# Attention and two MoE layers on one core: a third score group moved ahead, row gathers spread out, the last three feed-forward chunks grouped by tile

## The chip, the core and the metric

The kernel runs on one NeuronCore of a Trainium2 chip. Its engines work side by side, each on a queue of its own: TensorE (PE, matmuls; its weight loads are listed as PEld), VectorE (DVE), ScalarE (ACT), GpSimd (POOL) and SyncE (SP, which here only issues DMAs). Matmuls write into eight PSUM banks; DVE and ACT bring results from there to SBUF. The metric is the device time of one execution in microseconds (us); less is better. All times below are us unless marked ns.

## What is computed

Three stages follow one another. The inputs are q, k, v of 2 x 8 x 768 x 64, weights of 8 experts, and the two matrices of a feed-forward layer.

```python
# attention: a band of |i - j| < 16 beside 24 block summaries of 32 keys each
k_sum = k.reshape(B, H, nb, 32, D).max(axis=3)
v_sum = v.reshape(B, H, nb, 32, D).mean(axis=3)
scores_l = where(|i - j| < 16, scale * q @ k.T, -1e9)
scores_s = scale * q @ k_sum.T + log(32)
a = softmax(concat([scores_l, scores_s]))
x = (a @ concat([v, v_sum])).transpose(0, 2, 1, 3).reshape(1536, 512)
# experts: each row goes to the one expert with the largest logit
e = argmax(x @ w_gate, axis=1)
x = gate_w[:, None] * (relu(x @ w1[e]) @ w2[e])     # 512 -> 1024 -> 512
# feed-forward: 512 -> 2048 -> 512
h = x @ w_in
out = maximum(0.01 * h, h) @ w_out
```

## The kernel before

Products that need full precision are made of two rounded halves: an operand is split into a high part (cast on ACT) and a low part (the difference, on DVE), and three matmuls (high-high, high-low, low-high) replace one.

*Attention.* The 16 heads are worked as 8 pairs, each in two groups of six 64-row query tiles, so 16 groups n. A group runs through `scores` (PE: mask L325, products L337), `rowmax` (DVE L347), `weights` (ACT, exponentials L359), `turn_a` and `take_a` (PE transposes L368, ACT copy L372), `values` (PE L382) and `put_x` (DVE L394 to L405: division and the logits). Beside them, per pair, `project` (PE L305) makes the share of the logits that comes from the values, `project_t` transposes it (copy L309, transposes L313, copy L316), `mean_v` (PE L287) makes the block means of v, and `spread_v` (ACT L294) copies them behind each query tile's values. No loop sets the order. Each step is entered into a list `plan` with a due time (tables STAGE, EARLY and ONCE, L56 to L125, in units of one pair = 2), the list is sorted, and the steps are issued in that order; every engine works its own part of it in order.

*The first experts' rows.* `pick_rank`, `pick0` (L484 to L493), `pick1` to `pick3` and `pick_hot` choose, once the first 768 rows are known, the rows of the first two expert blocks (256 rows each); `pick_id` (L552) turns them by a matmul (L555) into a tile of row numbers `tid0` (DVE cast L558); `pick_x` (L560) gathers 128 rows each from the DRAM copy `xrows` with an indirect DMA (L561). All row copies into `xrows` (`put`, L417) and all gathers are issued by POOL. `b_turn` transposes the gathered rows of block 0; `b_l10` and `b_l11` are its first two units.

*The expert blocks.* A `Block` (L603) works on 256 rows of one expert, in eight units f of the hidden size: `load` (SP), `split` into halves, `layer1(f)` (L664, then ACT L670 and DVE L671), `layer2(f)` (L684), and at the end `store` (ACT L691, DVE L692). The first block has its order written out in the string POST (L130). Into it are mixed the five steps of `sort()`, which counts the rows of each expert (L803), finds each row's place (L820 to L827, one-hots L829 to L837), and turns that into the row numbers `tid` (PE L846, DVE cast L847), and then gathers all twelve tiles of 128 sorted rows (L849 to L857; L852 is the DMA). `list` works out which expert each later block has (L872 to L925), `zero` fills (L1116) the still unused part of x2h and x2l. From block 1 on `block()` (L1151) runs: in each unit it places two gathered tiles, `place` (L956), by PE transposes (L700) and copies, until all twelve are placed.

*Feed-forward.* Two halves of 768 rows, 16 chunks of the hidden size each, 32 chunks i in all. `ff1(i)` (L1233) makes the hidden chunk (L1243) and splits it (L1250 to L1253); `ff2(i, t)` (L1256) adds it to the output tile t, one of six (L1264). At the last chunk of a half the tile is evicted with its gate by ACT (L1272) or DVE (L1274), odd and even tiles in turn, and scattered to `out` by an indirect DMA of POOL (L1277). `ff2(i - 1, t)` runs behind `ff1(i)`; the last two chunks run together, tile by tile.

Of the kernel before, what the change touches and what calls it, by code (L numbers as in the profile page):

```python
# [11 lines left out]
I32 = mybir.dt.int32  # L12
ACTF = mybir.ActivationFunctionType
ALU = mybir.AluOpType
# [12 lines left out]
NJ = S // 128  # L27
# [5 lines left out]
NTT = TOK // 128  # L33
# [22 lines left out]
STAGE = {'b_hi': ([29.98, 30.98, 33.0, 34.4], 4),  # L56
 'b_lo': ([30.8, 30.8, 30.8, 30.8, 31.3, 31.3, 31.3, 31.3, 33.3, 33.3, 33.3, 33.3, 34.6, 34.6, 34.6, 34.6], 16),
 'pick_hot': ([25.4], 0.05),
 'pick_x': ([27.4], 0.1),
 'b_turn': ([32.1], 0.1),  # L60
 'load_k': ([-9.9], 4),
 'load_q': ([-9.85], 4),
# [18 lines left out]
 ('sum_v', 2): 2.9,  # L81
 ('mean_v', 0): 2.3,
 ('spread_v', 0): 2.32,
 ('spread_v', 1): 2.36,
 ('project', 0): 2.35,
 ('project_t', 0): 2.9,
 ('mean_v', 1): 4.9,
 ('mean_v', 2): 6.9,
 ('spread_v', 2): 4.97,
# [11 lines left out]
 'pick1': 22.9,  # L101
 'pick2': 23.3,
 'pick3': 24.9,
 'pick_id': 27.2,
 'b_load0': 23.1,
 'b_load1': 24.1,
 'b_load2': 25.0,
 'b_load3': 26.0,
 'b_l10': 34.0,
 'b_l11': 35.765,  # L110
 'wgi': -9.78,
 'cm': -1.0,
 'clear': 4.92,
# [14 lines left out]
 'place_g': 'p',  # L128
 'put': 'p'}
POST = (  # L130
    "load4 load5 load6 load7 put l1_2 sort sort l2_0 hi4 sort sort l1_3 l2_1 sort lo4 split5 l2_2 split6 l1_4 "
    "split1_x0 split1_x1 sort l2_3 split7 load1_0 load1_1 l1_5 zero l2_4 split1_0 load1_2 l1_6 list zero l2_5 "
    "split1_1 load1_3 load1_4 l1_7 list list zero l2_6 split1_2 l1_b1 list zero l2_7 list list pad store"
).split()
BUSY = [(-8.0, 6), (2.28, 5)]

# [2 lines left out]
def tile_kernel(  # L139
# [344 lines left out]
    def pick0():  # L484
        V = nc.vector
        V.tensor_copy(out=cnt0[:, 0], in_=rk0[:, NJ, :])
        V.tensor_reduce(out=top, in_=cnt0[:, 0], axis=AX.X, op=ALU.max)
        V.scalar_tensor_tensor(
            out=pe0[:, NJ, :], in0=cnt0[:, 0], scalar=top, in1=erev[:, NEARLY:NC], op0=ALU.is_ge, op1=ALU.mult
        )  # L490
        V.tensor_reduce(out=fs, in_=pe0[:, NJ, :], axis=AX.X, op=ALU.max)
        V.tensor_tensor(out=pe0[:, 0:NJ, :], in0=rk0[:, 0:NJ, :], in1=oh[:, 0:NJ, NEARLY:NC], op=ALU.mult)
        V.tensor_reduce(out=rank, in_=pe0[:, 0:NJ, :], axis=AX.X, op=ALU.add)  # L493

    def pick1():
# [62 lines left out]
        nc.vector.tensor_copy(out=tid0, in_=tp0)  # L558

    def pick_x(j):  # L560
        nc.gpsimd.indirect_dma_start(  # L561
            out=xr_t[0][:, j, :],
            out_offset=None,
            in_=xrows[0:S, :],
            in_offset=bass.IndirectOffsetOnAxis(ap=tid0[:, j:j + 1], axis=0),
        )

    def split_w(raw, hi, lo, eng=nc.vector):
# [228 lines left out]
    def sort():  # L797
# [47 lines left out]
        for n, j in enumerate(order):  # L845
            nc.tensor.matmul(out=tp, lhsT=am[:, j, :], rhs=bo[:, j, :], start=(n == 0), stop=(n == NTT - 1))  # L846
        V.tensor_copy(out=tid, in_=tp)  # L847

        for n, j in enumerate((0, 1, 4, 5, 6, 7, 8, 9, 10, 11, 2, 3)):  # L849
            if n == NTT - 2:  # L850
                yield
            nc.gpsimd.indirect_dma_start(  # L852
                out=xg_t[j],
                out_offset=None,
                in_=xrows[:, :],
                in_offset=bass.IndirectOffsetOnAxis(ap=tid[:, j:j + 1], axis=0),
            )  # L857

# [262 lines left out]
    def first_block(cur):  # L1123

        todo, blist = sort(), blocks()
        nxt = Block(1)
        ops = {
            "put": lambda: put(NB - 1, DM - 128, XW),
            "pad": lambda: nc.gpsimd.memset(xst[:, :, TOK:PADT], 0.0),
            "sort": lambda: next(todo, None),  # L1130
            "list": lambda: next(blist, None),
            "l1_b1": lambda: nxt.layer1(0),
            "store": lambda: cur.store(),
        }
        ops["zero"] = lambda: zeros.pop()()
        ops["hi4"] = lambda: cur.split_hi(4)
        ops["lo4"] = lambda: cur.split_low(4)
        for f in range(NF1):
            ops[f"load{f}"] = lambda f=f: cur.load(f)
            ops[f"split{f}"] = lambda f=f: cur.split(f)  # L1140
            ops[f"l1_{f}"] = lambda f=f: cur.layer1(f)
            ops[f"l2_{f}"] = lambda f=f: cur.layer2(f)
            ops[f"load1_{f}"] = lambda f=f: nxt.load(f)
            ops[f"split1_{f}"] = lambda f=f: nxt.split(f)
        for j in range(2):
            ops[f"split1_x{j}"] = lambda j=j: nxt.split_rows(j)
        for k in POST:
            ops[k]()
        return nxt

    def block(cur, nxt_b):  # L1151
# [4 lines left out]
        for f in range(1, NF1 + 1):  # L1156
# [12 lines left out]
            if f < NF1:  # L1169
                cur.layer1(f)  # L1170
            elif known and f == NF1:
                nxt.layer1(0)
            if turns:

                for _ in range(2):
                    place(turns.pop(0), cur.b)
                if zeros:
                    zeros.pop()()
# [46 lines left out]
    def feed_forward():  # L1225
# [7 lines left out]
        def ff1(i):  # L1233
            half = i // NF2
            hi, lo = fws[i]
            gh, gl = whi_b[i % 2][:, 0:HT], wlo_b[i % 2][:, 0:HT]
            for c in range(2):
                c0 = half * HT + c * CH
                ps = ps_f[c]
# [16 lines left out]
        def ff2(i, t):  # L1256
# [11 lines left out]
            if f == NF2 - 1:  # L1268
                j = (i // NF2) * NTH + t
                o = xst[:, t % KD, (t // KD) * DM:(t // KD + 1) * DM]  # L1270
                if t % 2:
                    nc.scalar.mul(out=o, in_=acc[t], mul=gate[:, j:j + 1])  # L1272
                else:
                    nc.vector.tensor_scalar(  # L1274
# [17 lines left out]
        for i in range(N2):  # L1292
            ff1(i)
            if i + 3 < N2:
                narrow(i + 3)
                if i + 5 < N2:
                    fraw[i + 5] = load_f(i + 5)
            if 1 <= i < N2 - 1:
                for t in range(NTH):
                    ff2(i - 1, t)  # L1300
            if i + 2 < N2:
                fws[i + 2] = split_f(fnar.pop(i + 2), i + 2)
        for t in range(NTH):
            ff2(N2 - 2, t)
            ff2(N2 - 1, t)

# [125 lines left out]
```

## Time and profile before

| | |
|---|---|
| time, median of 3 runs | 550.77 us |
| the three runs | 554.21, 550.77, 547.75 us |
| the profiled execution, its own time | 549.57 us |
| its span, first to last instruction | 547.4 us |
| PE busy | 515.5 us, 94% |
| DVE busy | 325.2 us, 59% |
| ACT busy | 272.9 us, 50% |
| POOL busy | 72.4 us, 13% |
| granted clock of PE, mean | 0.978 of full |
| moved by DMA | 90.10 MB, mean 165 GB/s |

How to read it: the profile is one execution taken by the hardware profiler. Each row of work names the engine, the line of the kernel, what it writes and reads, and, in brackets, how long the engine stood idle ahead of it and what released it ("issue" is time in which it waited for nothing that the profile shows, "remote" an unknown releaser). Consecutive instructions of one kind are one row with a count xN. Ends of matmuls are modelled, since they are pipelined. The granted clock is the share of full speed at which PE was allowed to run.

### The profile page before, as it was taken

The numbers are of one execution on the slowest core, as the hardware profiler recorded it, in microseconds if no ns is written. First come the engines' busy times: TensorE is split into PE (matmuls) and PEld (weight loads), VectorE is DVE, ScalarE is ACT, GpSimd is POOL, SyncE is SP. The second block draws the span as 40 slices with busy tenths as digits, with TensorE's granted clock in tenths as the row PEclk, the third lists the DMA queues.
The fourth block names the chain that finished last, engine by engine and source line by source line (L and its number), as shares of the span: only waits on it lengthen the run. The fifth ranks groups of instructions, "written<-read, shape, count | busy, mean of one in ns | idle before, by whom it ended". The sixth has DMA issues, their size and how long they took to land.

```text
span 547.4 us, 10508 instructions
## 1 busy us (share of the span) xinstructions
PE 515.5 (94%) x4139; PEld 461.6 (84%) x4139; DVE 325.2 (59%) x600; ACT 272.9 (50%) x479; POOL 72.4 (13%) x124
## 2 busy tenths in 40 slices
PE   6799878978999999999999999999999999999993
PEld 3467556967999999999999898998998989989882
DVE  3366758838576997684288877785444434334331
ACT  2688757437865676652155545444343333334331
POOL 0232360270000000000010110110022000000004
PEclk9899988997999999999999999999999999999998
DMA  8979774493467586565246645542224112122003
GB/s 264 294 229 289 208 253 137 138 352 132 153 222 250 186 305 222 174 224 193 91 180 230 223 166 189 207 162 95 77 78 154 57 59 78 38 78 77 2 0 120
DMA packets 23209, 90.10 MB, mean 165 GB/s; under 512 B 2800, under 2 KB 3312, under 8 KB 21104
## 3 DMA queue, kind: packets, MB, share of 16 engines
q1 hardware_dynamic: 15440, 53.58, 30.2%
q0 software_dynamic: 7712, 35.77, 18.4%
q8 instruction: 34, 0.56, 0.4%
q14 instruction: 23, 0.19, 0.1%
HBM read 74.61 MB, written 14.73 MB: 163 GB/s over the span
## 4 chain that ended last, share of the span: by engine, by line
PE 61%; issue 24%; DMA 4%; DVE 3%; ACT 3%; another core or an unknown queue 2%; POOL 2%; SPq 0%; ACTq 0%; POOLq 0%; DVEq 0%
PE bank L1243 13%; PE bank L684 12%; PE bank L1264 11%; PE bank L664 11%; DMA v<-in_vn_dram 2%; PE bank L337 2%; PE bank L368 2%; PE bank L382 2%; POOL out_dram L1277 2%; PE bank L1056 1%; PE bank L1046 1%; PE bank L700 1%; DMA vt<-in_vt_dram 1%; DMA mk<-in_cmask_dram 1%
## 5 line engine op out<-in xcount | busy, mean ns | idle before, releaser
L1243 PE MATMUL bank<-x2h,fwhi 128*128 128x384 f32 x256 | 86.9, 339 | 0.1
L1243 PE MATMUL bank<-x2l,fwhi 128*128 128x384 f32 x256 | 86.7, 339 | 0.0
L1243 PE MATMUL bank<-x2h,fwlo 128*128 128x384 f32 x256 | 86.7, 339 | 0.0
L1264 PE MATMUL bank<-fwhi,ewlo 128*128 128x512 f32 x192 | 76.0, 396 | 0.0
L1264 PE MATMUL bank<-fwlo,ewhi 128*128 128x512 f32 x192 | 75.8, 395 | 0.0
L1264 PE MATMUL bank<-fwhi,ewhi 128*128 128x512 f32 x192 | 75.7, 394 | 0.0
L570 DVE TENSOR_TENSOR ewlo<-eraw,ewhi 128x1024 fp32r<-128x1024 f32 x44 | 53.9, 1225 | 32.2 <-ACT ewhi L569 25.0
L570 DVE TENSOR_TENSOR fwlo<-fraw,fwhi 128x1024 fp32r<-128x1024 f32 x32 | 39.1, 1223 | 49.7 <-ACT fwhi L569 49.7
L569 ACT CAST fwhi<-fraw 128x1024 fp32r<-128x1024 f32 x32 | 33.6, 1050 | 52.3 <-PE bank L1264 52.3
L569 ACT CAST ewhi<-eraw 128x1024 fp32r<-128x1024 f32 x44 | 46.2, 1049 | 26.5 <-PE bank L684 21.8
L1253 DVE TENSOR_TENSOR ewlo<-eraw,ewhi 128x384 fp32r<-128x384 f32 x64 | 35.7, 558 | 37.1 <-ACT ewhi L1252 36.6
L664 PE MATMUL bank<-exl,ewhi 128*128 128x256 f32 x192 | 55.4, 289 | 2.3 <-issue 2.3
L1252 ACT CAST ewhi<-eraw 128x384 fp32r<-128x384 f32 x64 | 32.9, 514 | 48.5 <-DVE eraw L1251 48.5
L1250 ACT ACTIVATE eraw<-bank 128x384 f32<-128x384 f32 x64 | 31.4, 491 | 50.6 <-PE bank L1243 50.6
L684 PE MATMUL bank<-ehh,ewhi 128*128 128x256 f32 x192 | 56.0, 292 | 0.3 <-ACT ehh L670 0.3
L664 PE MATMUL bank<-exh,ewlo 128*128 128x256 f32 x192 | 55.1, 287 | 1.2 <-issue 1.1
L684 PE MATMUL bank<-ehl,ewhi 128*128 128x256 f32 x192 | 55.3, 288 | 0.2 <-issue 0.2
L664 PE MATMUL bank<-exh,ewhi 128*128 128x256 f32 x192 | 55.2, 287 | 0.0
L684 PE MATMUL bank<-ehh,ewlo 128*128 128x256 f32 x192 | 55.0, 286 | 0.0
L1251 DVE TENSOR_TENSOR eraw<-bank,eraw 128x384 f32<-128x384 f32 x64 | 35.7, 557 | 27.2 <-ACT eraw L1250 27.1
L1243 PEld LDWEIGHTS bank<-x2h,fwhi 128*128 128x128 f32 x256 | 48.0, 188 | 1.7 <-issue 0.3
L1243 PEld LDWEIGHTS bank<-x2l,fwhi 128*128 128x128 f32 x256 | 48.0, 188 | 1.6 <-DVE x2l L1080 0.2
(215 smaller groups left out, 985.9 us busy)
## 6 DMA issues: line engine op xcount, KB each, us to landing
eraw<-in_w_dram SPq DMA_DIRECT2D x52, 512.0 KB, 3.8
w<-in_wio_dram POOLq DMA_DIRECT2D x16, 1024.0 KB
wnar<-fraw POOLq DMA_DIRECT2D x16, 512.0 KB
fraw<-wnar SPq DMA_DIRECT2D x16, 512.0 KB, 3.4
v<-in_vn_dram SPq DMA_DIRECT2D x8, 657.0 KB, 9.2
k<-in_kt_dram SPq DMA_DIRECT2D x8, 400.0 KB, 6.1
vt<-in_vt_dram SPq DMA_DIRECT2D x8, 400.0 KB, 7.2
q<-in_qt_dram SPq DMA_DIRECT2D x8, 384.0 KB
```

The lines of the kernel that those rows point to most:

```text
L337: nc.tensor.matmul(out=s[h][e * QT:e * QT + QT, c:c + (NSUM if part else KWIN)], lhsT=q_b[p % NQ][r, t * QT:(t + 1) * QT], rhs=rhs, start= ...
L368: nc.tensor.transpose(ps_t[0:KW, i * 128:(i + 1) * 128], a[:, i, :], ident)
L569: nc.scalar.copy(out=hi, in_=raw)
L570: eng.tensor_tensor(out=lo, in0=raw, in1=hi, op=ALU.subtract)
L664: nc.tensor.matmul(out=ps, lhsT=w[:, k * 128:(k + 1) * 128], rhs=x[:, k, :], start=(n == 0), stop=(n == 3 * KD - 1),)
L684: nc.tensor.matmul(out=self.y[i // 2][:, i % 2, :], lhsT=w[:, c + i * 128:c + (i + 1) * 128], rhs=x, start=(f == 0 and n == 0 and i % 2 == ...
L1243: nc.tensor.matmul(out=ps, lhsT=w[:, k * 128:(k + 1) * 128], rhs=x[:, k, c0:c0 + CH], start=(n == 0), stop=(n == 3 * KD - 1),)
L1250: nc.scalar.mul(out=sm, in_=ps, mul=0.01)
L1251: nc.vector.tensor_tensor(out=g32, in0=ps, in1=sm, op=ALU.max)
L1252: nc.scalar.copy(out=gh[:, cs], in_=g32)
L1253: nc.vector.tensor_tensor(out=gl[:, cs], in0=g32, in1=gh[:, cs], op=ALU.subtract)
L1264: nc.tensor.matmul(out=acc[t], lhsT=g[:, t * 128:(t + 1) * 128], rhs=w[:, KD * 128:], start=(f == 0 and n == 0), stop=(f == NF2 - 1 and n ...
```

## The change

The change moves work in time; the arithmetic stays as it is.

- In the attention plan, the third group's `scores` go ahead of the first `values`, and `rowmax(1)`, `weights(2)` and `weights(3)` come earlier; the second `spread_v` goes later, behind the second `take_a`.
- `pick0` issues its product L492 right behind the copy L486. `pick_id` goes ahead of `turn_a` 25 and `put_x` 11.
- The four gathers `pick_x` get due times of their own (27.4, 28.5, 30.0, 31.2 in place of 27.4, 27.5, 27.6, 27.7). Each gets a copy of its column of row numbers in a tile of its own, made by DVE.
- `b_l11` goes ahead of `put_x` 15. In POST, `l2_0` goes ahead of the second `sort`.
- The twelve gathers leave `sort()`. Each is an operation `g` of its own, with a DVE copy of its column: eight of them stand between the layers of the first block in POST, and the other four in the first four units of block 1, each ahead of that unit's placing.
- In the feed-forward, the activations rotate over three buffers in place of two. The last three chunks, not two, run together tile by tile, and at the last chunk (i = 31) each eviction is shared: the first 256 columns on ACT, the last 256 on DVE.

```diff
--- before.py
+++ after.py
@@ -56,7 +56,7 @@
- 'pick_x': ([27.4], 0.1),
+ 'pick_x': ([27.4, 28.5, 30.0, 31.2], 4),
@@ -81,9 +81,13 @@
- ('spread_v', 1): 2.36,
+ ('spread_v', 1): 3.43,
+ ('scores', 2): 2.92,
+ ('rowmax', 1): 2.31,
+ ('weights', 2): 2.33,
+ ('weights', 3): 2.36,
  ('project', 0): 2.35,
- ('project_t', 0): 2.9,
+ ('project_t', 0): 2.85,
@@ -101,13 +105,13 @@
- 'pick_id': 27.2,
+ 'pick_id': 27.1,
...
- 'b_l11': 35.765,
+ 'b_l11': 35.1,
@@ -128,9 +132,9 @@
 POST = (
-    "load4 load5 load6 load7 put l1_2 sort sort l2_0 hi4 sort sort l1_3 l2_1 sort lo4 split5 l2_2 split6 l1_4 "
-    "split1_x0 split1_x1 sort l2_3 split7 load1_0 load1_1 l1_5 zero l2_4 split1_0 load1_2 l1_6 list zero l2_5 "
-    "split1_1 load1_3 load1_4 l1_7 list list zero l2_6 split1_2 l1_b1 list zero l2_7 list list pad store"
+    "load4 load5 load6 load7 put l1_2 sort l2_0 sort hi4 sort sort l1_3 l2_1 sort g lo4 split5 l2_2 g split6 l1_4 "
+    "split1_x0 split1_x1 g l2_3 split7 load1_0 load1_1 l1_5 g zero l2_4 split1_0 load1_2 l1_6 g list zero l2_5 "
+    "split1_1 load1_3 load1_4 l1_7 g list list zero l2_6 split1_2 l1_b1 g list zero l2_7 g list list pad store"
 ).split()
@@ -484,12 +488,12 @@
         V.tensor_copy(out=cnt0[:, 0], in_=rk0[:, NJ, :])
+        V.tensor_tensor(out=pe0[:, 0:NJ, :], in0=rk0[:, 0:NJ, :], in1=oh[:, 0:NJ, NEARLY:NC], op=ALU.mult)
...
-        V.tensor_tensor(out=pe0[:, 0:NJ, :], in0=rk0[:, 0:NJ, :], in1=oh[:, 0:NJ, NEARLY:NC], op=ALU.mult)
@@ -558,11 +562,14 @@
     def pick_x(j):
+        t = pre_p.tile([128, 1], I32, name=f"tid0_{j}")
+        nc.vector.tensor_copy(out=t, in_=tid0[:, j:j + 1])
         nc.gpsimd.indirect_dma_start(
...
-            in_offset=bass.IndirectOffsetOnAxis(ap=tid0[:, j:j + 1], axis=0),
+            in_offset=bass.IndirectOffsetOnAxis(ap=t, axis=0),
@@ -845,16 +852,21 @@
-        for n, j in enumerate((0, 1, 4, 5, 6, 7, 8, 9, 10, 11, 2, 3)):
-            if n == NTT - 2:
-                yield
-            nc.gpsimd.indirect_dma_start(
-                out=xg_t[j],
-                out_offset=None,
-                in_=xrows[:, :],
-                in_offset=bass.IndirectOffsetOnAxis(ap=tid[:, j:j + 1], axis=0),
-            )
+        yield
+
+    rows_left = [0, 1, 4, 5, 6, 7, 8, 9, 10, 11, 2, 3]
+
+    def gather():
+        j = rows_left.pop(0)
+        t = rt_p.tile([128, 1], I32, name=f"tid_{j}")
+        V.tensor_copy(out=t, in_=tid[:, j:j + 1])
+        nc.gpsimd.indirect_dma_start(
+            out=xg_t[j],
+            out_offset=None,
+            in_=xrows[:, :],
+            in_offset=bass.IndirectOffsetOnAxis(ap=t, axis=0),
+        )
@@ -1131,6 +1143,7 @@
+            "g": gather,
@@ -1170,6 +1183,8 @@
+            if rows_left:
+                gather()
             if turns:
@@ -1233,7 +1248,7 @@
-            gh, gl = whi_b[i % 2][:, 0:HT], wlo_b[i % 2][:, 0:HT]
+            gh, gl = whi_b[i % 3][:, 0:HT], wlo_b[i % 3][:, 0:HT]
@@ -1268,7 +1283,13 @@
-                if t % 2:
+                if i == N2 - 1:
+                    nc.scalar.mul(out=o[:, 0:DM // 2], in_=acc[t][:, 0:DM // 2], mul=gate[:, j:j + 1])
+                    nc.vector.tensor_scalar(
+                        out=o[:, DM // 2:], in0=acc[t][:, DM // 2:], scalar1=gate[:, j:j + 1], scalar2=None,
+                        op0=ALU.mult,
+                    )
+                elif t % 2:
                     nc.scalar.mul(out=o, in_=acc[t], mul=gate[:, j:j + 1])
@@ -1295,12 +1316,13 @@
-            if 1 <= i < N2 - 1:
+            if 1 <= i < N2 - 2:
                 for t in range(NTH):
                     ff2(i - 1, t)
...
         for t in range(NTH):
+            ff2(N2 - 3, t)
             ff2(N2 - 2, t)
             ff2(N2 - 1, t)
```

## Rows read from the trace of the kernel before

**Rows 1.** The page, part 1: busy time of each engine.

```profile
PE 515.5 (94%) x4139; PEld 461.6 (84%) x4139; DVE 325.2 (59%) x600; ACT 272.9 (50%) x479; POOL 72.4 (13%) x124
```

**Rows 2.** Order in time on PE: start, length, engine, line, names, idle before, releaser.

```profile
18.66 0.78 PE L325 MATMUL bank<-mk 128*128 128x360 bf16 x2
```

**Rows 3.** Order in time on ACT, same columns, 13 to 23 us.

```profile
13.39 0.87 ACT L294 COPY v<-bank 24x864 f32<-24x864 f32 x1 [1.14 <-PE bank L287]
...
18.53 1.62 ACT L359 ACTIVATE a<-bank,nm 128x120 f32<-128x120 f32 x6
22.77 0.34 ACT L309 COPY vp<-bank 128x224 f32<-128x224 f32 x1 [2.61 <-PE bank L305]
```

**Rows 4.** Busy time by stretch, with PE clock, DMA share, GB/s.

```profile
core 0: us, PE busy (x) PEld busy (x) DVE busy (x) ACT busy (x) POOL busy (x), PEclk, DMA share, GB/s
15.06:18.48 3.42, 1.76 (x21) 1.09 (x19) 0.95 (x1) 2.15 (x5) 0.00 (x0) 0.99 1.00 227
18.48:21.89 3.41, 3.41 (x59) 2.35 (x55) 0.59 (x2) 1.67 (x7) 0.00 (x0) 0.51 1.04 396
83.30:86.70 3.40, 3.19 (x24) 2.05 (x24) 2.36 (x18) 2.80 (x9) 0.00 (x0) 0.50 0.17 66
106.40:112.24 5.84, 5.84 (x52) 5.84 (x52) 4.86 (x6) 3.73 (x6) 4.62 (x5) 1.00 0.62 205
112.24:135.33 23.09, 17.38 (x101) 15.30 (x99) 12.82 (x56) 12.03 (x16) 10.08 (x21) 0.78 0.69 246
116.00:120.90 4.90, 2.84 (x15) 1.94 (x15) 0.00 (x0) 0.40 (x1) 3.78 (x4) 0.99 1.02 391
120.90:131.10 10.20, 8.27 (x35) 7.31 (x34) 7.14 (x35) 6.63 (x9) 3.46 (x14) 0.50 0.55 182
```

**Rows 5.** Order in time on DVE and PE at 60 us.

```profile
60.03 0.20 DVE L492 TENSOR_TENSOR pe<-bank,oh 128x48 f32<-128x48 f32 x1
...
60.38 0.41 PE L287 MATMUL bank<-wgi,vs 128*24 128x144 f32 x2 [1.13 <-DVE pe L492]
```

**Rows 6.** Order in time on PE at 76 us.

```profile
75.84 0.58 PE L305 MATMUL bank<-vt,wgi 128*32 128x224 f32 x8 [1.01 <-DVE tid L558]
```

**Rows 7.** Order in time on PE, DVE and POOL, 78 to 83 us.

```profile
78.47 0.36 PE L337 MATMUL bank<-ks,q 64*64 64x24 f32 x8
...
82.14 0.53 DVE L347 TENSOR_REDUCE m<-bank 128x3 f32<-128x360 f32 x1 [6.36 <-remote]
...
81.12 0.95 POOL L561 DMA_INDIRECT xr<-xrows,tid  x1 [0.30 <-issue]
```

**Rows 8.** Order in time on POOL and PE, 106 to 136 us.

```profile
106.40 1.74 POOL L852 DMA_INDIRECT xr<-xrows,tid  x1 [4.26 <-DVE tid L847]
...
121.00 0.95 POOL L852 DMA_INDIRECT xr<-xrows,tid  x1 [0.30 <-issue]
...
135.33 0.93 PE L700 MATMUL bank<-ident,xr 128*128 128x128 f32 x5 [1.73 <-DVE x2l L692]
```

**Rows 9.** Waits of DVE, 105.9 to 136 us: total, times, longest.

```profile
DVE ewlo L570 <- issue: 6.6, 1, 6.6
DVE ehl L671 <- ACT ehh L670: 2.8, 2, 1.8
DVE ewlo L570 <- ACT ewhi L569: 1.3, 2, 1.0
```

**Rows 10.** Order in time on ACT and POOL at the end.

```profile
538.94 0.69 ACT L1272 ACTIVATE xst<-bank,gate 128x512 f32<-128x512 f32 x1 [2.12 <-issue]
540.08 0.96 POOL L1277 DMA_INDIRECT out_dram<-xst,tid  x1 [0.30 <-issue]
```

**Rows 11.** Order in time on PE and DVE, 100 to 106 us.

```profile
100.44 0.64 PE L803 MATMUL bank<-lt,cm 128*128 128x10 f16 x12 [1.03 <-DVE lt L455]
...
103.35 1.96 DVE L837 TENSOR_TENSOR am<-cm,posf 128x384 f16<-128x384 f16 x4
```

**Rows 12.** Groups of instructions of ACT, 105.9 to 136 us: busy, mean ns, idle before.

```profile
L1116 ACT CAST x2l<-cv 128x1536 fp32r<-128x1536 f32 x4 | 5.9, 1465 | 0.0
```

**Rows 13.** DMA traffic, 108 to 126 us.

```profile
DMA packets 1669, 5.80 MB, mean 322 GB/s; under 512 B 269, under 2 KB 269, under 8 KB 1668
...
q0 software_dynamic: 960, 3.20, 48.8%
```

## The prediction

> **What bounds the kernel now.** I began with the page's busy shares: TensorE (PE) is busy for 94% of the span [rows 1]. So an edit gains only where PE stands still or runs at half clock, or at the very end. The chain that ended last, the waits by engine and the order in time then gave five such places; from 136 us on PE runs without a gap up to the last scatters.
>
> *Start.* The third score group (L325, L337) starts at 18.66 [rows 2]. ACT then waits 2.61 us, until 22.77, for the projection that comes behind those scores [rows 3]. PE was busy for 1.76 of the 3.42 us before 18.48, and the 3.41 us after that ran at a granted clock of 0.51 [rows 4]: the lower of its two levels, 1.2 of 2.4 GHz.
>
> *Two short waits for DVE.* At 60.38 PE waits 1.13 us for a product (L492) that reads the PSUM bank PE wants [rows 5]; at 75.84 it waits 1.01 us for the cast of the picked ids (L558) [rows 6].
>
> *First gather burst.* POOL issues a put and four indirect DMAs (L561) back to back, to 82.07. PE's score matmuls are recorded up to 78.83, yet DVE's reduction of them starts at 82.14, after 6.36 idle us [rows 7]. The releaser is "remote": nothing that the profile knows. Work that was finished was not announced.
>
> *Second gather burst.* POOL issues twelve indirect DMAs (L852), the first at 106.40, the last from 121.00 to 121.95 [rows 8]. Up to 112.24 PE is busy without a gap and DVE for 4.86 of 5.84 us; from 116 to 120.9 PE works 2.84 of 4.9 us and DVE not at all; then PE runs at 0.50 to 131.1 [rows 4]. DVE's waits there are 6.6, 2.8 and 1.3 us [rows 9]. PE's last wait, 1.73 us at 135.33, is for the store of block 0 on DVE [rows 8]: there DVE is the bound.
>
> *End.* PE's last matmul ends at 538.90; ACT evicts it from 538.94 for 0.69 us, but its scatter is issued only at 540.08: POOL issues one per 1.26 us without a pause [rows 10].
>
> **The change, part by part.** Negative is a gain.
>
> *Scores early: -1.6.* ACT's two sets of weights move ahead of the second spread, which goes behind the second take. The first spread ends at 14.26; six exponentials take 1.62 and the projection copy 0.34 [rows 3], so 16.2. I let project_t wait for all of that and give its transposes 0.7: scores(2) at 16.9 against 18.66, 1.8 earlier. The next projection is held by the put-off spread: the scores end at 18.5 at the full clock (half of 3.41), then a transpose, six value pairs, take and spread to 20.4, projection to 21.2; ACT resumes there instead of at 22.77, 1.6 earlier. Bounds: 0.8, if the half-clock stretch comes again and takes 0.9 back; 2.2, if project_t waits for its copy alone.
>
> *Product ahead in pick0: -0.5.* L492 passes three small operations (L487 to L491) of about its own 0.20 us [rows 5], 0.6 in all; 0.3 if they overlap by half.
>
> *pick_id ahead of put_x(11): -0.4.* The cast passes put_x's four operations. The wait is 1.01 us, but PE's transposes (L368) now stand behind the one-hots from POOL, so I take under half. Bounds 0.2 and 0.6.
>
> *Picked rows spread: -3.3.* Each gather gets its own cast of one column on DVE, and POOL waits for that; what is queued behind on POOL are only puts. On DVE nothing stands between the casts of gathers 0 and 1 (only PE and ACT work is planned between due times 27.4 and 28.5). So put, gather 0 and gather 1 stay back to back; gather 2 waits for the prefix sums, gather 3 for put_x(13), and b_turn needs only rows 0 and 1. If the silence ends with the last issue of the burst (82.14 against POOL's 82.07), it now ends two issues of 1.25 earlier: -2.5. If two gathers cause none: DVE starts 3.2 earlier, at 78.9, and half of the 3.19 busy us of PE at clock 0.50 behind it [rows 4] comes back, 1.6: together -4.8. The put is unchanged, so I stay near the first. Gather 3 stands right behind the put of put_x(13); a silence of one issue, 1.25, would be the worst there; taken as 0.
>
> *layer2(0) ahead of the last counts, b_l11 ahead of put_x(15): 0.* PE's 1.03 us wait at 100.44 is filled with layer2's matmuls. But PE next needs the one-hots, which DVE finishes at 105.31 with its 1.96 us of L837 [rows 11]; DVE has no gap there, so PE waits at L846 instead. The work that hides the gain is DVE's; without it the gain is 1.03. The moved `ehl` (L671) ran ahead of L820 anyway.
>
> *Counted rows spread: -7.0.* Eight of the twelve gathers are issued between layers, one per 2 to 4 us where it was 1.25, and four in block 1. POOL has little else to do meanwhile. DVE's order sets block 0's store. DVE waits 6.6 + 2.8 + 1.3 = 10.7 us on the way there [rows 9]. Of this I leave 2.0: ACT's fills of 1.47 us [rows 12] stand ahead of casts that DVE needs. Eight new casts cost about 0.08 each, half of a small operation, since these overlap: 0.7. So the store comes 10.7 - 2.0 - 0.7 = 8.0 earlier, and PE's place at 127.3 instead of 135.33. I take 7.0, since weight loads and gathers still meet from 107 to 112. Bounds 3.3 (the transfers bind, below) and 8.0. The four casts and gathers in block 1 cost nothing: PE bounds that stretch. Without that cover they cost their 0.3 us.
>
> *Clock: +0.8.* From 112.24 to 135.33 PE was idle for 23.09 - 17.38 = 5.7 us, and its 8.3 busy us at clock 0.50 [rows 4] would be 4.1 shorter. So PE would be ready at 125.5 and wait 1.8 us for the store. After the stretch with 1.76 busy us of 3.42 the clock fell to 0.51 for 3.41 us [rows 4]. If it does here, that costs 1.7. Taken at half; bounds 0 and 1.7.
>
> *Feed-forward end: -0.4.* The matmuls are the same, and the third buffer for the activations removes no wait (PE has none there). Three chunks per tile put nine matmuls, 2.1 us, between two tiles, more than POOL's 1.26, so the last scatter no longer queues. Half an eviction lies between half of 0.69 and 0.69; I take 0.45. With POOL's 0.30 ahead of an issue [rows 10]: 538.94 + 0.45 + 0.30 = 539.69, against 540.08. Bounds 0.2 and 0.6.
>
> Sum: -1.6 - 0.5 - 0.4 - 3.3 - 7.0 + 0.8 - 0.4 = -12.4. The profiled execution took 549.57 (span 547.4 and 2.2 around it), 1.2 below the median 550.77 and inside the shown 547.75 to 554.21. Forecast 537.2.
>
> **Rivals.**
>
> *The transfers bind (541.4).* From 108 to 126 us 5.8 MB moved, 3.20 of them in POOL's queue, at 322 GB/s [rows 13], with a DMA share of 1.02 from 116 to 120.9 [rows 4]. If DVE and ACT wait there for bytes, only the four gathers that leave count: 4 x 0.27 MB at 322 GB/s, 3.3 us. Two gathers less in the first burst, 0.53 MB at a like rate, give 1.7 to 2.0; I take 2.0. Sum: -1.6 - 0.5 - 0.4 - 2.0 - 3.3 - 0.4 = -8.2. For it: the share. Against it: PE stalls within a group whose operands have all arrived.
>
> The Trainium skill ("DMA: Bandwidth & Descriptors", section on issuing engines that are not separate DMA queues) says that transfers of all issuers run on the same 16 engines and interleave. By that rule spreading removes no byte, and the sum is this rival's 541.4, not 537.2. The trace is against it so far: the finished matmuls that nobody heard of are no transfer.
>
> *A price per gather, not per burst (546.6).* Each of the sixteen gathers silences the engines for a while, wherever it stands. Then only the start, the two short waits and the end remain: -1.6 - 0.5 - 0.4 - 0.4 = -2.9; with the bounds of these four, -1.5 to -4.0, 545.6 to 548.1. For it: both bursts show it. Against it: the first gathers of the second burst, up to 112.24, delayed neither PE nor DVE [rows 4].
>
> *The other side: a lone gather costs more (557.7).* In the first burst four gathers cost DVE 6.36 us, 1.6 each; in the second twelve cost about 8, 0.7 each, because they overlap. If a lone one costs 1.6, sixteen lone ones cost 25.4 against 14.4 now: +11.0 - 2.9 = +8.1. It gets slower than before from (14.4 + 2.9) / 16 = 1.1 us per gather. Block 1 with its four gathers, PE-bound today, would show it first.
>
> **How the numbers follow.** Forecast 0.58, transfers bind 0.19, price per gather 0.15, lone gathers dear 0.08. Within the forecast the bounds run from 533 (all large gains, no clock loss: -2.2 - 0.6 - 0.6 - 4.8 - 8.0 - 0.6 = -16.8) to about 541. With the first rival, 533 to 545 holds 0.77; up to 546 it takes in the favourable edge of the second, 0.03 more: 0.80. About 1% (5.5 us) is what a measurement of this kernel can tell from no change: forecast and first rival are faster than that (0.77), the second is within it (0.15), the third is slower (0.08).
>
> **What would show it.** In the profile after: scores(2) at about 17, and no half-clock stretch there; PE's waits at L287 and L305 under 0.7; no "remote" wait of over 3 us at L347; no wait inside a group of L664; the first place of block 1 some 12 us earlier in all; an interval of 0.8 us between the last matmul and the last scatter. If place comes only 5 to 8 us earlier, the transfers bind; if "remote" waits appear beside lone gathers or in block 1, one of the last two rivals holds. The forecast is wrong if the silence belongs to something that the bursts only accompany, or if DVE's order in block 0 binds harder than its waits say.

## The result, and the profile after

The changed kernel takes 536.46 us (median of four runs, 534.8 to 537.25) against 551.0 for the kernel before (547.75 to 554.21): a ratio of 0.9717, 95% interval 0.9676 to 0.9757. The forecast was 537.2. The gain is 14.5 us where 12.4 were forecast. The total is right; most of it came from where the prediction put it, but one of its foundations does not hold on every chip, as the experiments show.

The profiled execution after took 534.8 us. The page, part 1, busy time of each engine, to be held against [rows 1]:

```profile
span 532.7 us, 10506 instructions
...
PE 507.9 (95%) x4139; PEld 456.8 (86%) x4139; DVE 326.8 (61%) x619; ACT 273.5 (51%) x482; POOL 74.1 (14%) x124
```

PE does the same 4139 matmuls in 7.6 us less busy time. Fewer of them ran at half clock (the mean granted clock is 0.988, before 0.978), and 1.1 us of the 7.6 lie in the feed-forward. The other half of the gain is PE's idle time. Four landmarks of the two traces, and the gaps between them, say where it went:

| from, to | before | after | difference |
|---|---|---|---|
| start of the trace to ACT's first spread of means (13.39, 12.61) | 13.39 | 12.61 | -0.78 |
| to the cast of the picked row numbers (75.64, 71.13) | 62.25 | 58.52 | -3.73 |
| to the cast of the counted row numbers (105.96, 98.74) | 30.32 | 27.61 | -2.71 |
| to the first place of block 1 (135.33, 120.30) | 29.37 | 21.56 | -7.81 |
| to the end of the span (547.4, 532.7) | 412.07 | 412.40 | +0.33 |

The rows behind these landmarks that are not shown elsewhere, first two of before, then two of after:

```profile
75.64 0.15 DVE L558 CAST tid<-bank 128x4 int32<-128x4 f32 x1
105.96 0.17 DVE L847 CAST tid<-bank 128x12 int32<-128x12 f32 x1 [0.31 <-PE bank L846]
```

```profile
12.61 0.87 ACT L298 COPY v<-bank 24x864 f32<-24x864 f32 x1 [1.11 <-PE bank L291]
71.13 0.15 DVE L562 CAST tid<-bank 128x4 int32<-128x4 f32 x1
```

The second line of the table is one pair of executions. The same stage takes 58.52, 65.70 and 62.06 us in three traces of the changed kernel (after, again, again2) and 62.25 and 66.00 in two of the kernel before (before, before2), so its 3.73 us cannot be put down to the change alone. The last line is a sum too: +1.31 from the first place to the first matmul of the feed-forward (L1243 before, L1258 after), -1.07 from there to the last matmul, +0.09 behind it.

*The start.* Order in time on PE and on ACT, after, where [rows 2, 3] have 18.66 and 22.77:

```profile
14.66 0.53 PE L317 MATMUL bank<-ident,vp 128*96 128x128 f32 x3
15.03 0.47 PE L329 MATMUL bank<-mk 128*128 128x360 bf16 x2
```

```profile
19.25 0.35 ACT L313 COPY vp<-bank 128x224 f32<-128x224 f32 x1 [0.89 <-PE bank L309]
```

The third scores start at 15.03, right behind the transposes of project_t at 14.66. ACT's wait for the next projection falls from 2.61 to 0.89 in this pair of traces.

*The short waits and the picked rows.* Order in time on PE, POOL and DVE, after, where [rows 5 to 7] have waits of 1.13, 1.01 and 6.36:

```profile
57.06 0.41 PE L291 MATMUL bank<-wgi,vs 128*24 128x144 f32 x2 [0.48 <-DVE pks L492]
...
71.64 0.59 PE L309 MATMUL bank<-vt,wgi 128*32 128x224 f32 x8
```

```profile
74.28 0.37 PE L341 MATMUL bank<-ks,q 64*64 64x24 f32 x8
```

```profile
75.15 0.99 POOL L568 DMA_INDIRECT xr<-xrows,tid  x1 [0.30 <-issue]
```

```profile
76.53 0.97 DVE L351 TENSOR_REDUCE m<-bank 128x3 f32<-128x360 f32 x2 [4.13 <-PE bank L386]
```

DVE still stands still for 4.13 us, and again until just after the last gather issued back to back, the second here (75.15 + 0.99 = 76.14). Not all of it is silence: the scores that DVE reads end on PE at 74.65, so 1.88 us are, where before it was 3.31 (78.83 to 82.14).

*Block 0.* Order in time on DVE and PE, after; then busy time by stretch; then the waits of DVE from 99 to 124 us, which answer to [rows 9]:

```profile
98.74 0.17 DVE L854 CAST tid<-bank 128x12 int32<-128x12 f32 x1
```

```profile
120.30 1.97 PE L707 MATMUL bank<-ident,xr 128*128 128x128 f32 x8 [3.18 <-DVE x2l L699]
```

```profile
108.00:112.00 4.00, 4.00 (x36) 4.00 (x35) 3.46 (x14) 3.62 (x6) 0.95 (x2) 1.00 0.91 315
112.00:116.00 4.00, 4.00 (x35) 4.00 (x34) 3.90 (x24) 3.81 (x5) 0.95 (x1) 1.00 0.82 254
120.40:123.50 3.10, 3.10 (x15) 3.10 (x16) 2.60 (x5) 1.96 (x2) 1.65 (x2) 0.51 0.63 178
```

```profile
DVE ewlo L577 <- ACT ewhi L576: 2.4, 2, 1.6
```

DVE's 10.7 us of waits are 2.4, and PE has no gap until it waits 3.18 us for the store. Behind that wait the clock does fall, to 0.51 for 3.1 us.

*The end.* Order in time on PE, ACT, DVE and POOL, after, where [rows 10] have 538.94 and 540.08:

```profile
523.71 0.40 PE L1279 MATMUL bank<-fwhi,ewlo 128*128 128x512 f32 x1
```

```profile
524.15 0.47 ACT L1287 ACTIVATE xst<-bank,gate 128x256 f32<-128x256 f32 x1 [1.63 <-PE bank L1279]
...
524.65 0.48 DVE L1288 TENSOR_SCALAR xst<-bank,gate 128x256 f32<-128x256 f32 x1 [1.62 <-ACT xst L1287]
...
525.42 0.96 POOL L1298 DMA_INDIRECT out_dram<-xst,tid  x1 [1.14 <-POOLq L1330]
```

The two halves run one after the other: DVE starts at 524.65, when ACT has ended at 524.62, and its releaser is ACT. From the last matmul's end (524.11) to the last scatter it is 1.31 us, where it was 1.18.

### The profile page after: what moved, and what is told of

The parts are those of the page before. It is cut to its first block, busy times and chain, and to the rows that moved or that the text cites. A ratio compares the mean times of both kernels' runs of the same rounds, so it can differ in the third digit from the quotient of the medians.

```text
span 532.7 us, 10506 instructions
## 1 busy us (share of the span) xinstructions
PE 507.9 (95%) x4139; PEld 456.8 (86%) x4139; DVE 326.8 (61%) x619; ACT 273.5 (51%) x482; POOL 74.1 (14%) x124
## 5 line engine op out<-in xcount | busy, mean ns | idle before, releaser
L1258 PE MATMUL bank<-x2h,fwhi 128*128 128x384 f32 x256 | 86.6, 338 | 0.1
L1258 PE MATMUL bank<-x2l,fwhi 128*128 128x384 f32 x256 | 86.6, 338 | 0.0
L1258 PE MATMUL bank<-x2h,fwlo 128*128 128x384 f32 x256 | 86.5, 338 | 0.0
L577 DVE TENSOR_TENSOR ewlo<-eraw,ewhi 128x1024 fp32r<-128x1024 f32 x44 | 53.9, 1224 | 27.6 <-ACT ewhi L576 27.1
L671 PE MATMUL bank<-exh,ewhi 128*128 128x256 f32 x192 | 54.6, 284 | 0.0
L671 PE MATMUL bank<-exh,ewlo 128*128 128x256 f32 x192 | 54.4, 283 | 0.0
L671 PE MATMUL bank<-exl,ewhi 128*128 128x256 f32 x192 | 54.3, 283 | 0.0
L1258 PEld LDWEIGHTS bank<-x2h,fwhi 128*128 128x128 f32 x256 | 48.1, 188 | 1.6 <-issue 0.3
L1258 PEld LDWEIGHTS bank<-x2l,fwhi 128*128 128x128 f32 x256 | 48.1, 188 | 1.4 <-DVE x2l L1092 0.2
```

The lines of the kernel that those rows point to most:

```text
L577: eng.tensor_tensor(out=lo, in0=raw, in1=hi, op=ALU.subtract)
L671: nc.tensor.matmul(out=ps, lhsT=w[:, k * 128:(k + 1) * 128], rhs=x[:, k, :], start=(n == 0), stop=(n == 3 * KD - 1),)
L1258: nc.tensor.matmul(out=ps, lhsT=w[:, k * 128:(k + 1) * 128], rhs=x[:, k, c0:c0 + CH], start=(n == 0), stop=(n == 3 * KD - 1),)
```

## The experiments

The theory on trial: a train of indirect DMAs on POOL holds back what the other engines hear of each other. The rivals: the bytes of the transfers bind; the gathers' own tiles, not their spacing, took the waits away; and, from the second chip on, that the waits came by chance or with the chip. Twelve runs were made on four more chips, each timed against the kernel before on the same chip; no chip was used at two times, so what belongs to the chip and what to the moment cannot be told apart here. "Cast to place" is the time from the cast of the counted row numbers to the first place; "wait" is DVE's longest idle time ahead of a row maximum (L347 or L351) at the picked rows.

| chip | before, us | run | ratio to before, interval | wait | cast to place |
|---|---|---|---|---|---|
| the result | 551.0 | before | 1 | 6.36 | 29.37 |
| | | changed | 0.9717 (0.9676 to 0.9757) | 4.13 | 21.56 |
| 1 | 538.86 | burst12 | 1.0308 (1.0234 to 1.0381) | 2.74 | spoilt |
| | | direct12 | 1.0207 (1.0121 to 1.0292) | 1.25 | spoilt |
| | | pickburst | 0.9964 (0.9923 to 1.0005) | 1.12 | 21.56 |
| | | oldstart | 1.0006 (0.9961 to 1.005) | 2.11 | 21.57 |
| 2 | 554.58 | again | 0.9642 (0.955 to 0.9734) | 4.31 | 21.56 |
| | | burst10 | 0.9809 (0.973 to 0.9887) | 4.34 | 29.13 |
| | | onlypost | 0.981 (0.9709 to 0.991) | 5.80 | 21.56 |
| | | best | 0.9715 (0.9645 to 0.9785) | 3.55 | 20.90 |
| 3 | 538.09 | before2 | (540.01, one run) | 2.16 | 21.22 |
| | | direct10 | 0.9903 (0.9865 to 0.9941) | 1.24 | 21.65 |
| | | best2 | 0.9895 (0.9852 to 0.9937) | 1.30 | 18.55 |
| 4 | 539.54 | again2 | 0.994 (0.9904 to 0.9975) | 1.24 | 21.56 |

**All twelve counted rows back to back, indirect and plain (burst12, direct12).**

```diff
-            "g": gather,
+            "g": lambda: [gather() for _ in range(len(rows_left))],
 # direct12 besides:
-        nc.gpsimd.indirect_dma_start(out=xg_t[j], ..., in_=xrows[:, :], in_offset=...)
+        ...  # POOL copies the first column of row numbers, so that it starts behind the same cast
+        nc.gpsimd.dma_start(out=xg_t[j], in_=xrows[j * 128:(j + 1) * 128, :])
```

direct12 leaves out the choice of rows: it moves 128 rows in their order.

> The changed kernel with all twelve counted-row gathers issued back to back at the place of the first one (each still with its own copy of its column on DVE). Silence theory (a train of indirect DMAs on POOL holds back what the other engines hear of each other until its last issue): about 8 us slower than the changed kernel, 544 to 545; DVE and ACT wait over 5 us in block 0, PE stalls within a group of layer matmuls, the first place comes at about 128 where it was 120.3. Transfer theory (only the four gathers that left block 0 counted): 3.3 us slower, 540. Tile theory (the gathers' own tiles of row numbers, not the spacing, took the waits away): no change, 536.5.

> As burst12, but the twelve transfers are plain DMAs of POOL's queue of 128 rows in their order, the same bytes and the same row length, started by the same cast (so the rows are not those of the experts; the work behind them is the same in amount). Silence theory, tied to the indirect form: no wait over 2 us on DVE in block 0, first place at about 121, 537. Transfer theory: as burst12, since the bytes and their moment are the same. A third, a train of any DMAs of POOL silences: also as burst12, with the silence ending at the last issue.

Both were slower, but they tell nothing of the theory: gathers 2 and 3 write the tile from which block 1's rows are still to be transposed, and in my order these transposes came to depend on the last two gathers. PE waited 16.8 us for that landing in the one and 11.6 in the other. The kernel before keeps these two back for this reason, and burst10 and direct10 do so again.

**The picked rows back to back again (pickburst).**

```diff
- 'pick_x': ([27.4, 28.5, 30.0, 31.2], 4),
+ 'pick_x': ([27.4, 27.5, 27.6, 27.7], 4),
```

> The changed kernel with the four gathers of the picked rows back to back again (due 27.4 to 27.7), each still with its own copy. Silence theory: DVE's wait ahead of its score reduction grows from 4.1 to 6.4 us and more, ends with the fourth issue, and 2.5 to 3.3 us are lost: 539 to 540. Transfer theory: 2.0 us, 538.5. Tile theory: no change.

The time, 536.89 us, is what the tile theory said, though the changed kernel was not run on this chip. A wait shorter than the changed kernel's 4.13 us no theory had. The train of a put and four gathers is there, to 78.16, and DVE's reduction starts in its midst, after 1.12 us. Order in time on POOL and on DVE:

```profile
72.10 0.92 POOL L421 DMA_DIRECT2D xrows<-xr  x1 [2.01 <-DVE tid L567]
...
77.21 0.95 POOL L568 DMA_INDIRECT xr<-xrows,tid  x1 [0.30 <-issue]
```

```profile
73.17 0.97 DVE L351 TENSOR_REDUCE m<-bank 128x3 f32<-128x360 f32 x2 [1.12 <-PE bank L341]
```

And the kernel before took only 538.86 us on this chip, 12 less than in the result. From here the question was whether the waits belong to the kernel at all.

**The start undone (oldstart).** The tables of before for spread_v, scores, rowmax, weights and project_t of the first pair.

> The changed kernel with the start's due times of before (scores, row maxima, weights, second spread and project_t of the first pair). By the two traces the start is worth 2.7 us (ACT resumes at 19.25 against 22.77, less the 0.8 us by which the traces already differ ahead of it): 539.2, with a stretch at clock 0.5 at about 18 us. Rival: a later wait for loads takes the gain back, since the first pairs' inputs still arrive: 537.

On its chip the whole rest of the change then brings nothing that can be told from noise (1.0006), while the changed kernel is at 0.994 of before on another such chip (again2): 0.7%, some 3.6 us, for the start, with intervals that leave 0.5 to 7. On the same chip as oldstart, pickburst with the new start has 0.9964: 0.4%, not clear of the noise. So a gain of the start is likely, and its size is open. Loads can take it back, as the rival had it: in the trace of `again` (an execution of 541.42 us) the early scores wait 2.03 us for the load of q, and half clock follows with the new order too. Order in time on PE, and busy time by stretch, again:

```profile
15.63 0.60 PE L341 MATMUL bank<-k,q 64*64 64x96 f32 x8 [2.03 <-DMA q<-in_qt_dram]
```

```profile
17.50:21.00 3.50, 3.50 (x28) 2.18 (x28) 1.71 (x4) 1.35 (x2) 0.00 (x0) 0.50 1.02 342
```

In oldstart the half clock did not come at this place. Busy time by stretch, oldstart, against [rows 4]:

```profile
15.00:18.50 3.50, 1.82 (x16) 0.97 (x17) 0.82 (x1) 1.91 (x4) 0.00 (x0) 1.00 1.01 228
18.50:22.00 3.50, 3.50 (x82) 2.37 (x82) 1.26 (x4) 2.02 (x8) 0.00 (x0) 1.00 1.02 354
```

The same old order with the same thin stretch (1.82 of 3.50 busy) leaves the clock at 1.00 here; before it was 0.51 afterwards. That loss is not a fixed price of the order.

**The change again, the train again, and its second part alone (again, burst10, onlypost).**

```diff
 # burst10: ten back to back at the first place, two behind split1_x
-            "g": gather,
+            "g": lambda: [gather() for _ in range(gaps.pop(0))],
+        gaps = [10, 0, 2, 0, 0, 0, 0, 0]
 # onlypost: the kernel before with POST, g, sort() and block() of after, and nothing else
```

> The changed kernel itself once more, in the same call as the next three, so that they can be compared on one chip. If the gain is the same on every chip: 0.972 of the kernel before. If it hangs on the chip or on how the single execution falls: nearer to 1.

> The changed kernel with the counted-row gathers issued as before: ten back to back at the first place, the last two behind the transposes of block 1's rows (so that nothing waits for a tile still in use, which spoilt the run with all twelve); each still has its own copy of its column. Silence theory: 7 to 8 us slower than the changed kernel, DVE's waits in block 0 add up to some 10 us, PE stalls within a group of layer matmuls. Tile theory (the copies, not the spacing, took the waits away): as the changed kernel. Chance theory (the waits of the one profiled execution before came by chance, as those at the picked rows did): as the changed kernel within 2 us, with waits under 3 us.

> The kernel before with the second part of the change alone: the order of POST with the spread gathers and layer 2 ahead of the last counts, and the four gathers in block 1. By the two traces this part is worth 7.8 us net of the rest: 543 where the kernel before takes 551. If start and picked rows are worth nothing, as the runs that undid them say, this part holds nearly all of it: 537 to 538. If it is worth nothing either: 550.

On this chip the train does bring the waits. burst10 keeps the casts and the own tiles and changes the spacing (POOL issues all twelve in one train, to 122.48): 29.13 us from cast to place where `again` has 21.56, and 1.7% of the time, some 9 us, with intervals that leave 2.5 to 16. So the tiles were not it. Order in time on DVE and PE, again and then burst10:

```profile
104.20 0.17 DVE L854 CAST tid<-bank 128x12 int32<-128x12 f32 x1
125.76 1.97 PE L707 MATMUL bank<-ident,xr 128*128 128x128 f32 x8 [3.17 <-DVE x2l L699]
```

```profile
102.44 0.17 DVE L854 CAST tid<-bank 128x12 int32<-128x12 f32 x1
131.57 1.27 PE L707 MATMUL bank<-ident,xr 128*128 128x128 f32 x8 [1.82 <-DVE x2l L699]
```

The waits of DVE and PE in burst10, 102.4 to 132 us, show the mark of [rows 9] again:

```profile
DVE ewlo L577 <- issue: 4.7, 3, 2.3
DVE ehl L678 <- ACT ehh L677: 3.9, 1, 3.9
```

```profile
PE bank L691 <- ACT ehh L677: 3.0, 1, 3.0
PE bank L671 <- issue: 2.4, 3, 1.0
```

onlypost has all the 21.56, so the second part alone carries it: 1.9% of the gain of 3.6% on this chip. Its picked rows, untouched, still cost 5.80 us. Order in time on DVE, and on PE:

```profile
82.21 0.53 DVE L347 TENSOR_REDUCE m<-bank 128x3 f32<-128x360 f32 x1 [5.80 <-remote]
```

```profile
128.65 1.25 PE L700 MATMUL bank<-ident,xr 128*128 128x128 f32 x8 [3.17 <-DVE x2l L692]
```

**The kernel before once more, profiled (before2).**

> The kernel before, profiled once more. In the call with pickburst and oldstart it took 538.9 us, in the others 551 to 555, and the waits around the picked rows were shorter in that call's traces. If the waits come and go with the chip: either about 538 with DVE's wait ahead of L347 under 2 us and 22 us from the cast of the row numbers to the first place, or about 552 with over 5 us and 29 us; nothing between.

This is the run that decides. On a chip where it takes 540.01 us, the twelve gathers follow each other as ever, the last issued at 121.83, and the waits of [rows 9] are gone: DVE has 2.7 us of waits in all. Order in time on POOL, DVE and PE; then the stretch from 116 to 120.9, whose row of before is in [rows 4]; then all waits of DVE from 105.7 to 127:

```profile
121.83 0.94 POOL L852 DMA_INDIRECT xr<-xrows,tid  x1 [0.30 <-PE bank L684]
```

```profile
105.76 0.17 DVE L847 CAST tid<-bank 128x12 int32<-128x12 f32 x1 [0.32 <-PE bank L846]
```

```profile
126.98 0.90 PE L700 MATMUL bank<-ident,xr 128*128 128x128 f32 x3 [3.02 <-DVE x2l L692]
```

```profile
116.00:120.90 4.90, 4.90 (x43) 4.90 (x42) 4.69 (x22) 4.77 (x5) 3.99 (x4) 1.00 1.01 402
```

```profile
DVE ewlo L570 <- ACT ewhi L569: 2.4, 2, 1.6
DVE tid L847 <- PE bank L846: 0.3, 1, 0.3
```

The DMA share is 1.01 at 402 GB/s, as full as in the trace of before (1.02, 391), and PE works 4.90 of 4.90 us where it worked 2.84; DVE 4.69 where it did nothing. So the transfers do not bind: the same bytes in the same moment delay nobody, and in the trace of before they moved at a like rate while PE and DVE stood still. And the train alone is not enough either. Cast to place is 21.22 us with twelve in a row, a little less than the 21.56 with them spread.

**Plain transfers in the train (direct10).** burst10 with the plain DMA of direct12.

> As burst10, but the twelve transfers are plain DMAs of POOL's queue, 128 rows in their order each, the same bytes and row length, started by the same cast (the rows are not those of the experts; the amount of work behind them is the same). On a chip with the waits: if they belong to the indirect form, no wait over 2 us on DVE in block 0, 22 us from cast to first place, as the changed kernel; if they belong to the bytes or to any train of DMAs on POOL, 27 us and more, as burst10 (29.1).

21.65 us and 0.9903. But this chip showed no waits with the indirect form either, so the run does not tell the forms apart. That stays open.

**Two versions meant to be faster (best, best2).**

```diff
 # best: pick_x as in pickburst; whole evictions at i == N2 - 1; in POST
-... l1_b1 g list zero l2_7 g list list pad store
+... l1_b1 g list zero l2_7 g store list list pad
 # best2: whole evictions; pick_x due 27.4, 28.8, 30.8, 32.2; in POST
-... l2_6 split1_2 l1_b1 g list zero l2_7 g list list pad store
+... l2_6 l1_b1 g zero l2_7 g store split1_2 list list list pad
```

> The changed kernel with three things altered: picked rows back to back, block 0's store ahead of the last two steps of the list (DVE's 2.3 us of small operations there stand ahead of the store that PE waits 3.18 us for), and whole evictions in the last chunk (the two halves ran one after the other). By the trace: 2.2 us for the store, some of the 1.6 us of half clock behind it, 0.2 for the evictions, 0 to 2 for the picked rows: 2.5 to 5 us faster than the changed kernel. Rival: PE's wait moves to the next place in block 1, and only 1 us is left.

> The changed kernel with every picked row's gather on its own (each behind other work of DVE), block 0's store ahead of the split that block 1 needs later and of the last three steps of the list, and whole evictions in the last chunk. From cast to first place 21.6 - 3.2 = 18.4 us, no half clock behind it (1.6), DVE's wait at the first picked row 4.1 to about 2, 0.3 at the end: 4 to 7 us faster than the changed kernel, 530 to 534 where the kernel before takes 551. Rival: the wait moves to the split that now stands behind the store, and 2 us are left; with a train of put and one gather the silence is as long as with two.

best gains 0.66 us from cast to place, not 2.2: the longer of the last list steps (L924 to L938) stood ahead of the store still. Its ratio is not better than that of `again`: it ran on the chip with the waits and had the picked rows in one train (3.55 us). There the wait outlasts the train, whose last issue ends at 79.23, and PE itself stands still inside its scores. Order in time on PE and DVE, best:

```profile
80.12 0.32 PE L341 MATMUL bank<-k,q 64*64 64x96 f32 x1 [1.14 <-issue]
81.58 0.97 DVE L351 TENSOR_REDUCE m<-bank 128x3 f32<-128x360 f32 x2 [3.55 <-PE bank L372]
```

Its whole eviction does what the halves did not. Order in time on ACT and POOL, best:

```profile
525.13 0.69 ACT L1287 ACTIVATE xst<-bank,gate 128x512 f32<-128x512 f32 x1 [3.51 <-PE bank L1279]
```

```profile
526.10 0.96 POOL L1292 DMA_INDIRECT out_dram<-xst,tid  x1 [1.08 <-POOLq L1324]
```

The last matmul ends at 525.10 there, so the interval is 1.00 us, 0.31 less than in the changed kernel. best2 moves the store ahead of these steps and of a split. Order in time on DVE and PE:

```profile
114.33 1.29 DVE L699 TENSOR_TENSOR x2l<-bank,x2h 128x512 fp32r<-128x512 f32 x2 [0.36 <-ACT x2h L698]
```

```profile
115.07 1.25 PE L707 MATMUL bank<-ident,xr 128*128 128x128 f32 x8 [0.17 <-DVE x2l L699]
...
121.44 0.66 PE L707 MATMUL bank<-ident,xr 128*128 128x128 f32 x4 [1.81 <-DVE xst L248]
```

From cast (96.52) to place 18.55 us, and PE's wait is 0.17 where it was 3.18. 1.81 of that come back one place later, at 121.44, behind the split and the list steps that were put off; so the rival expectation was half right. 0.9895 on a chip without the waits stands beside 0.994 of the changed kernel on another such chip; the intervals overlap, and direct10, which has none of these alterations, is at 0.9903 on the same chip as best2. That best2 is the faster one is not shown.

**The changed kernel on one more chip (again2).**

> The changed kernel against the kernel before, on whatever chip this call falls. On a chip where the kernel before takes about 552: 0.964 to 0.972 of it, 4 us of DVE's wait at the picked rows. On a chip where it takes about 538 (no such waits there): the counted rows and the picked rows bring nothing, so only the start, the two short waits and what the store's new place in time costs are left: 0.99 to 1.0, 533 to 538; 21 to 22 us from the cast of the row numbers to the first place on either.

The second case: before takes 539.54, the change brings 0.6%. On the two chips with the waits it brings 2.8 and 3.6%.

## Why the prediction was right, and where it was not

The time hit closer than the sum. The gain was 2.1 us larger than forecast, and the sum began from an execution of 549.57 us, 1.4 below the median that the result is held against; that these two in part cancel is luck.

*Scores early, -1.6.* ACT resumed 3.52 us earlier, 2.7 without the 0.78 that the traces differ ahead of it. For this pair the term was too small: project_t waited for its own copy alone (its transposes at 14.66, behind a copy from 14.26), the case that I had as the bound of 2.2, and no half clock came. From ACT's first spread to its copy of the next projection it is 6.63 or 6.64 us in seven of the ten traces with the new start, and 7.57, 7.91 and 10.70 in the others; the four with the old start have 7.87, 9.36, 9.38 and 10.39. So it is 1.2 to 3.8 us in the seven, and nothing in again (10.70), where a load came late.

*The two short waits, -0.9.* L492 ahead: the wait went from 1.13 to 0.48, -0.65 against -0.5. pick_id: the 1.01 us at L305 are gone, but PE now waits 0.92 and 0.40 ahead of the matmuls of pick_id, where it had 0.35 and 0.24; what is left is about -0.3 against -0.4, as the working said.

*Picked rows, -3.3.* The stage shrank by 2.71 us. Put and the first two gathers did stay back to back, and the wait did end with the last issue; it was 4.13 us where 3.9 would have followed, 1.88 of them silence. What the spacing is worth by itself is less than the term: on the chip with `again`, the stage from the picked to the counted cast takes 27.79 us there, 28.83 in best with all four in one train, and 30.83 in onlypost with neither spacing nor own tiles. By these single traces the spacing brings about 1 us; the other 2 come with the own tiles or the place of pick_id, which no run separates.

*layer2(0) first, 0.* Right: onlypost has it and has the whole stage from picked to counted cast at 30.83 us, against 30.32 of before; on the chips without waits the stage is 25.01 with the whole change (again2) and 24.82 without (before2).

*Counted rows, -7.0, and the clock, +0.8.* -7.81 up to the first place, near the bound of 8.0. DVE still waits 2.4 us for ACT's casts, a little more than the 2.0 that I left, so the new casts cost less than the 0.7. The clock did fall behind PE's wait for the store: 3.1 us at 0.51, so about 1.5 of the 1.7 that I had as the upper bound.

*The end, -0.4.* Wrong in sign, +0.13. The step that failed is "half an eviction": I had both halves run at once. DVE waits for ACT. The Trainium skill ("PSUM — Partial Sum Buffer", section on PSUM bank collisions) says that no two engines may access one bank in the same partitions at once, reads included, so that their accesses have to be ordered by semaphores; the trace agrees (DVE's releaser is ACT, 0.03 us between the halves), and the rule should have been in the working: 0.47 + 0.48 for the halves against 0.69 for the whole. Both halves also go into one tile, xst; no run tells whether the bank or the tile ordered them.

The working also took the feed-forward's matmuls as the same, and there a cost may have been missed. From its first to its last matmul the feed-forward takes 269.26 or 269.27 us in all eleven traces with the grouped chunks and the third buffer, and 267.77 in the two others without them (onlypost, before2). The page, part 5, after and then before2:

```profile
L1258 PE MATMUL bank<-x2h,fwhi 128*128 128x384 f32 x256 | 86.6, 338 | 0.1
L1243 PE MATMUL bank<-x2h,fwhi 128*128 128x384 f32 x256 | 85.9, 336 | 0.2 <-ACT x2h L1079 0.2
```

The trace of before has 270.33 us and 339 ns, so that the pair of the result shows a gain of 1.07 us here. Which of the two is the rule, and why the same program has 336 and 339 ns, stays open.

*The rivals.* Transfers bind: refuted by before2; a full DMA share was just no wait. The rule that the prediction cites from the Trainium skill ("DMA: Bandwidth & Descriptors", section on issuing engines that are not separate DMA queues), that all issuers share the same engines, is not touched by it. A price per gather, and lone gathers dear: refuted by the changed kernel itself, which has four gathers in block 1 and no wait of PE behind the store. (The time of the former adds up to 546.7, not 546.6.)

*What the prediction did not see.* It took the waits of one profiled execution for a property of the kernel. The step that does not hold in general is "if the silence ends with the last issue of the burst": the silence is there on two chips and missing on three, with the same instructions in the same order (before and before2). Where it is missing, both gather terms (-10.3 together in the forecast) are about nothing, and what is left of the change is little more than its start. The forecast hit because the result was measured on a chip of the first kind. What makes a chip one or the other stays open: the runs show the same instructions and the same bytes on either kind. That the releases of finished work are held up at all is inferred from the engines' waits; no row shows the place where they are held. It is also not the whole of it: PE stands still inside groups of matmuls, where the profile shows nothing to wait for (2.4 us at L671 in burst10, and before, order in time on PE):

```profile
122.57 0.57 PE L664 MATMUL bank<-exl,ewhi 128*128 128x256 f32 x1 [1.03 <-issue]
```

If the engines got their instructions late, it could look the same; that rival is untested.

## What to carry to other kernels

Spread a train of indirect DMAs over other work of the issuing engine where that costs nothing: for the counted rows it was worth about 8 us on some chips and cost 0.3 on the others. Before a wait with no releaser ("remote", "issue" in the midst of a group) is put into a sum, profile the same kernel on a second chip. And do not halve the eviction of one PSUM bank between two engines; give whole banks in turn (1.00 us from last matmul to last scatter against 1.31).

## What the runs showed of the hardware

- The same kernel takes 551 to 555 us on some chips and 538 to 540 on others; in the two traces of it, the two stages with trains of indirect DMAs on POOL differ by 5.5 us (30.32 against 24.82) and 8.2 us (29.37 against 21.22).
- A DMA share of 1.01 at 402 GB/s left PE, ACT and DVE all above 95% busy (before2, 116 to 120.9 us).
- After a stretch with PE half idle (1.76 of 3.42 us busy, and 1.82 of 3.50) the granted clock fell to 0.51 in one execution (before) and stayed at 1.00 in the other (oldstart).
- A half eviction of 256 columns took 0.47 us on ACT and 0.48 on DVE, a whole one of 512 on ACT 0.69 (after, best).
